# Turning a quad of tokens by a transfer or by TensorE, and a new order of steps

## The chip, the cores and the metric

The kernel runs on one core of one Trainium2 chip. The metric is the device time of one execution in microseconds (us); several executions are timed and the median counts. A profile of one more execution shows what each engine did: TensorE (PE, and PEld for its weight loads), VectorE (DVE), ScalarE (ACT), GpSimd (POOL) and SyncE (SP, which here only issues transfers). PSUM is the memory that matmuls write; SBUF holds everything else on the chip.

## What is computed

An attention block over four batches of 12416 tokens of 128 channels with 32 inducing points, twice (the points attend to the tokens, then the tokens to the 32 results `h`), and a feed-forward layer with a ReLU gate on the tokens.

```
def mab(q, kv):
    s = scale * (q @ kv.transpose(0, 2, 1))
    s = s - s.max(-1, keepdims=True)
    a = np.exp(s)
    a /= a.sum(-1, keepdims=True) + 1e-09
    return a @ kv
h = mab(I, x)                      # I: 32 points for each of 4 batches
x = mab(x, h)                      # (4, 12416, 128), then as (49664, 128)
gate = np.maximum(x @ w_gate, 0.0) # w_gate, w_val: 128 x 1536
val = x @ w_val
out = gate * val @ w_out           # w_out: 1536 x 128
```

## The kernel before

The second attention and the feed-forward layer are folded: since a token's attention output is a mixture of 32 rows of `h`, the layer's output is a quadratic form in its 32 weights `p`. For each batch the kernel makes tables `T` and `L` out of `h` and the weights, and per token it needs only `p`, the squares `F` of differences of pairs of `p`, and matmuls of `F` and `p*p` with the tables. A last check at the end branches to a general kernel, which does not run for these inputs.

A batch has 97 tiles of 128 tokens: six *quads* of 16 tiles and a *rest* of one tile. Each batch has a first phase (needs every token of it once, gives `h` and the tables) and a second (gives the outputs, one block `Q` for a quad).

- First phase of batch 0: `first_batch`, before everything else, about the first 25 us. It loads x as fp32, casts it, turns each group of eight tiles by PE transposes (L336) and copies them out of PSUM on DVE (L337).
- First phase of batches 1 to 3, by quad: `load` (L206, a transfer on POOL's queue that casts to fp16 into one of six buffers `x16q`, or `x16r` for the rest), `turn` (L664, a transposing transfer on SP's queue from `x16q` to one of twelve buffers `xT`), `s1` (scores, PE L673), `p1` (exp, ACT L678), `hz` (weighted sums, PE L688), `ha` (added up, DVE L711). After the rest come `join` and `centre`, which give `h`, then the tables: `gate`, `u` (products `U`, DVE L876), `uj` (their join, L890, DVE or POOL or left to PE), `tm` (PE L895), `tab` (L909 or L907).
- Second phase, by block `Q`: `s2` (PE L472), `p` (exp, ACT L481), `pp` (squared p, L491, DVE or POOL), `z` and `zr`, `zq` (sums and reciprocals), for j = 0 to 3 `d` (differences, 16 matmuls in all, L528), `f2` (squares of two banks, ACT L542) and `fc` (the other two: squared by ACT L554, or cast by DVE L556 and then multiplied, `fm`, L560, by DVE or POOL), then the outputs `o` (PE L568 and L580), `e` (divide into one of four buffers `osb`, DVE L590), and `st` (store, SP L605).

No scheduler runs on the chip: the order is a text, `ORDER`, which names one step after another, its engine where it has several, and the buffer of each ring (`m`, six PSUM banks; `F`, twelve; `xT`; `x16`; `osb`) that it takes. `Plan.run` issues them in that order. Each engine works off its own instructions in this order and waits at each for what it needs; what stands behind on the same engine waits too. SP's queue holds loads of batch 0, turns and stores; POOL's holds the loads of batches 1 to 3. A batch's loads stand on POOL behind `turned` (L660), a copy of one element that waits for the transposing transfers of the batch before. A step `turn` of a quad is allowed only after the turn of the quad before, and quad 0's only after the rest's:

```
before = [("after", "turn", b, q - 1 if q else NQ)] if q < NQ else []
add(("turn", b, q), "SP", [("load", b, q)] + before, xs + xs2, f(turn, q))
add(("s1", b, q), "PE", [("turn", b, q)], xs2 + [p1, ms], f(s1, q))
```

Of the kernel before, what the change touches and what calls it, by code (L numbers as in the profile page):

```python
# [10 lines left out]
FP16 = mybir.dt.float16  # L11
# [5 lines left out]
class Plan:  # L17
# [9 lines left out]
    def add(self, name, engs, deps, uses, fn, unless=None):  # L27
        engs = (engs,) if isinstance(engs, str) else tuple(engs)
        self.steps.append((name, engs, list(deps), list(uses), fn, unless))

    def run(self, text, idle):
# [3 lines left out]
        left = {}  # L35
# [6 lines left out]
        def over(s):  # L42
            for k in s[3]:
                left[k] -= 1
                if not left[k]:
                    used.remove((k[0], self.slot[k]))

        def dropped():
# [25 lines left out]


ORDER = """
Ls00Lt2Lo050q040Lu2Lp2000320r1011Lq2Lz022S011Lw04L-1Lx1Ly1Lr2M12Lv20t05030304202200600030M922T1L+10
810710A1MA2M820ID041BM320K10J10CD020A0u2MF2MB20D10G1MM0MN03MG0MH04ME2MC2MD2MI0MJ00O00509MO00E10M10P
1MP0M230Q2MY0MS0MT02MK00w00158MQ0ML10R30530v3M43MR20y20x1MZ04MU0MV01C00317MW00S10+2Ma0M5001D11G1MX2
0-31E216005261711F2Mb01A21e032Mc0Md1M6210001251221f1M711111810U040V00k031B30s32KE40l02V002W21410m00  # L80
n01q001541r11u10Z001h020o20Jm460W0440300a01330z30b01i24510c01k002531s11g210d230X0Jr471I031l11J01Y01
1o20Y21m21Z02000052Jw481T041a01n31j32112412221b02331p30f02J-490g01U047001c221w005111V01x11y24821+10
h01K00i0K44A0j24931N051W01O0Jn000K94BJo11X21z22e001201L01P01Q0Js0142f12g2Jp001R21Jq21M2Jt12k001592i
11S40e4Ju04Jx00026022B030p42l12m12o2Jy12C04A0051AM022p2Jv22U203G0424C24B1K00104E13H1K11270Jz05J+24D
2K50012Y0054BK61K2002c12Z12D0280K701Me22X2K32KA014K823I222a1KF000KM32902E0KG12q00157KN30KB12A212r12
s12u12M00KT312F2KC04KH022N02O0KD22G4KI23M003482P02H01KJ22Q23KZ322h346313N1KK02Kf332I0KL22J03O13Q13Y
005052-032K03Z13c13a13003102L2320Kl34Kr35Mj04Mq023320Ms1Mr1Mf01Mn00Mk2Mp1Mo1Ml23503360Mg2Mm2Mh23703
e005262w04M-2Mi2Mv2Mw22x03i13f12y03802z03A003J02Mu13g12+23B03C0Mx3Kx33442R43D03S0014239213K23T13L33
E23U13W14SB05334T14U14W1N02Mt2N22My026W0013+013-03v04Mz2N126X1ND23w04G005344I13x04004105i002M+14K1N
724H1NE056Z02NF06a2NI15j1N803N904M00251NC14O13y03p004u0303q0N32N42N62N524Q14N13F4Ky41d44v13r03k023s  # L90
03l03m03z20422KO413n05400537NJ24Y044Z0NP35515814a04b0NK013o23NL05615G003294o05KU40Ka43434NO13t24c21
5H14p04q04r05I15A000105k304d04Kg424s225C24e04w225D34f04g04j035K15B15E14+0052BKm454h25225014-14x004k
0NQ01NR0533KP014NU24y24i4Ks447K0504z2KQ15o002165X005p17L15s24l04m05M045N05q24n25t35u00128KR055O05v1
KV003KS25y25P0KW15w15R055l025Y05Q20Kb0135S0Kc164004155T05m25n25r26826515U05Z0KX025V25z35+00312661KY
25W44t4Kd053u46Y21622Kh0025a05c045-1601Ke2Kn011633Ki16i005335d0Ko15e05f07N026j16m1880126925b216k2Kj
006Q056l3Kk27O28916o0030AKp02Kt0016R06S0L436p16T0L5306s25g25h46u000416U20NV2Kq2Ku16q16L016v17P2Kv03
6M06N06c005246O06y16w16A046g26P2Kw26d1Kz0106B0LB316t36C06D0K+16e17c002196E226V46F007d1LH326h36G06H0
K-037e28y0517g16b3L02L126I07Q0042B8z17R17U17S1L2036J2L3279017A08A32LN33LT347M307B07C07W005007E027D2
38-047F0NW039027a17Y18B007G0Ne01NZ2NX27H07X1913LZ35Na04Nh058C2NY27I27f3Lf3Ng1Nf17300Nb2Nc2Nd27i0031
7Nj1Ni1Nu26+026-07j1700710740Nl375072217608E005457m17k19m0107728F17t027J46K47847u08I17v0Ny28Q003027  # L100
o047w09n18U18G18R17p07z017+07-07q0Nm2Nv2Ns2Nt27r08S19800058800N+3991O40O5037x207s2O60O709C19A18K002
46O808M28L1Lg49p0582008308409q28O18W002518N2Nn2O92850No2N-04L6488123862O008Y18a18X18D3Np03CC022LC47
Nq2Nw2O319K00514CD1Nr19L18s008h048i08j0LI468k0Nz2Nx29M19O1A20023A8t08u08v08n058o0LO498l22OA38p0A31A
61A418w218q0L7001874LU4A9E00403L818c03Lh0129I28r29G19F1L9018d0La4B8e0LA2LD000OG29J38+318f09y00457LE
1OB01Li19+29z17y4LF008x4OC08g2A01LJ0029200439LG2942OF2LK1OH00931OI0CF05Aa021LL04CG29529619s00150Ab1
LM29Q039w29t19u2LP0049R09S0LQ1Ay0025B9v3CH3OL29b01Az1B029T0LR009U239o20LS2A+1Ag004519c0Ah19d09V03Ai
29e0Ad02Ak19x2A8000459W0Ae2AA2AC19X09Y0A91BO050Aj2Ac329Z2Lj02LV0049g00BP1Af29-2AB2Lb013LW19r39h09i0
Lc19j09f20BU00546LX039k2BV1AE01LY28m49a49l4AF0BY2AG0BW1AH0As00032AI21Ld04At1AP05Le2AQ0Nk2Lk2AR0Au1A
m00144Ll2AS0AJ02An1Aq2AK0AT22AL0Ar2B13AM0Bg00048Aw1Ao1Bi2AN2AU05Bh1AV0AW0AX0D0031Bk1Ba00109B702D11B
b1Be1AY2OM2BQ21D230B80B90BI04BA0Bc1Bm00533BJ0BB23Bj2BK0BL0Bn1Bo1Bq1D300BM20BR01B202B30B40D42BS2B50B  # L110
T2D52CU00405BZ3B62Lm01CV1CW2Dq050BC4AO4BD03Ln2Dr1CI00247BE0CY1BF0CE32CX3BG0BH2CK1CJ1CM2OR05OV00ON01
OX1OW1CO00230OO2OS2CN3OY04Bs00OP2OU2OT2CP1Bt0OQ2Bu0Oc3Oa1OZ1CQ2Bv0D60051ACS1Bw23C604C70C102D71Oo2C8
0Ca0030BOj2D81DA1C90C20Cb1C30Ee052CR3C40CA21Ce2Ef1E000144C52Cf3Bx00E11E22CB4Dt05By0Eh02Bz0Cc1Du2B+0
Ok2Ei2Eq00151E41Cl03Cg04Er1B-2Ch0Om2Cm0Eu1Es1DO00202Ci0Oe3DS2Cj0DP1Cn0Co0Cr05Ck21Ol2DQ1DI00103Cw04D
J1Cp2Cx0Cy0Or2Cz0Cs0DK1AZ4C04Cq4DC00239DM1Ct0DG2Cu0DD1Cv22Os01Ot0FS001DE1Dv3Od3DT3Ow2Dw00356Ox0C+2F
# [21 lines left out]
def square_body(ctx, tc, x, inducing, moe_w_gate, moe_w_val, moe_w_out, out):  # L137
    nc = tc.nc
    B, N, C = x.shape
    M = inducing.shape[0]  # L140
    DFF = moe_w_gate.shape[1]
    P = 128
# [5 lines left out]
    NQ = NT // CT  # L148
# [24 lines left out]
    eye16 = const([P, P], FP16, "eye16")  # L173
# [24 lines left out]
    x16q = [const([P, CT, C], FP16, f"x16q{i}") for i in range(NX16)]  # L198
    x16r = [const([P, 1, C], FP16, f"x16r{b}") for b in range(B)]
# [236 lines left out]
    mb = [psum.tile([P, BLK], FP32, name=f"mb{i}") for i in range(NM)]  # L436
# [13 lines left out]
    seen16 = mt([P, 1], FP16, "seen16")  # L450
# [11 lines left out]
    def xT_of(b, q):  # L462
        return xTq[slot["xT", b, q]] if q < NQ else xTr[b]
# [140 lines left out]
        t0 = q * CT + 8 * h  # L604
        nc.sync.dma_start(out=ov[b][:, t0 : t0 + 8, :], in_=o)  # L605

    for Q in range(B * NQ + 1):
        rest = Q == B * NQ
        b, q = divmod(Q, NQ)
# [2 lines left out]
        def f(g, *a, Q=Q):  # L612
            return lambda e: g(Q, *a, e)

        js = range(1 if rest else 4)
        src = [("turn", i, NQ) for i in range(1, B)] if rest else [("turn", b, q)]
# [39 lines left out]
    def load(b, q, e):  # L656
        load_x(b, q, x16q[slot["x16", b, q]] if q < NQ else x16r[b])

    def turned(b, e):
        pool.tensor_copy(out=seen16, in_=xT_of(b, NQ - 1)[:, 0, 0:1])  # L660

    def turn(b, q, e):
        src = x16q[slot["x16", b, q]] if q < NQ else x16r[b]
        nc.sync.dma_start_transpose(out=xT_of(b, q), in_=src.rearrange("p t c -> p (t c)"))  # L664

    def x16_of(b, q):
        return x16q[slot["x16", b, q]] if q < NQ else x16r[b]
# [67 lines left out]
    for b in range(1, B):  # L735
# [4 lines left out]
        for q in range(NQ + 1):  # L740
# [537 lines left out]
```

## Time and profile before

| | us |
|---|---|
| median of 3 executions | 266.23 (264.77 to 266.80) |
| the profiled execution, its own time | 266.63 |
| its span, first to last instruction | 264.8 |
| PE busy | 236.7 |
| DVE busy | 211.8 |
| ACT busy | 207.1 |
| POOL busy | 105.2 |

Busy times are unions over the span, and an engine that is full in one stretch can be idle in another, so views by stretches of time say more than these shares. Matmuls are pipelined, and PE's busy time counts the time until each one's end; it is not a measure of how fast matmuls could follow each other. The second table is of the transfers that matter here.

| transfer | queue | count | us from issue to landing, median |
|---|---|---|---|
| store of an `osb` (512 KB) | SP | 48 | 4.2 |
| load of a quad (512 KB) | POOL | 18 | 13.3 |
| load of a rest (32 KB) | POOL | 3 | 15.3 |
| turn of a quad | SP | 18 | 5.4 |
| turn of a rest | SP | 3 | 3.2 |

### The profile page before, as it was taken

How to read it: one execution, taken by the hardware profiler on the slowest of the kernel's cores; microseconds unless marked ns; L12 is line 12 of the kernel's file. 1: busy time of each engine (PE TensorE's matmuls, PEld its weight loads, DVE VectorE, ACT ScalarE, POOL GpSimd, SP SyncE). 2: the span in 40 equal slices, each digit the busy share in tenths (PEclk: the TensorE clock that was granted, in tenths of full speed). 3: DMA queues.
4: the chain of work that ended last, by engine and by line, in shares of the span. 5: the costliest groups of instructions: out<-in, count | busy, mean ns of one | idle time of the engine just before them, and what ended most of it. 6: DMA issues, size and time to landing. Idle time of an engine off the chain costs nothing.

```text
span 264.8 us, 9054 instructions
## 1 busy us (share of the span) xinstructions
PE 236.7 (89%) x3835; PEld 170.4 (64%) x3835; DVE 211.8 (80%) x439; ACT 207.1 (78%) x382; POOL 105.2 (40%) x132
## 2 busy tenths in 40 slices
PE   6798889997999788689999499999999999999991
PEld 2686367775767566457777367766666767777780
DVE  3656986784899936568999457999999999989993
ACT  3565979788989667379999568899999999989820
POOL 4457337402620715037604443105450774535100
PEclk9999999999999979799999979999999999999998
DMA  7995995999999669999999599922153214454463
GB/s 256 422 412 137 210 213 110 171 188 261 224 242 274 172 161 178 238 255 243 266 255 249 100 178 229 369 93 112 49 231 136 116 79 162 175 223 161 158 244 125
DMA packets 52620, 53.46 MB, mean 202 GB/s; under 512 B 41280, under 2 KB 41952, under 8 KB 52576
## 3 DMA queue, kind: packets, MB, share of 16 engines
q1 hardware_dynamic: 47952, 42.90, 55.6%
q0 software_dynamic: 4576, 9.93, 20.2%
q8 instruction: 31, 0.51, 0.8%
q14 instruction: 13, 0.11, 0.1%
q10 hardware_dynamic: 48, 0.02, 0.1%
HBM read 27.80 MB, written 25.43 MB: 201 GB/s over the span
## 4 chain that ended last, share of the span: by engine, by line
PE 42%; DMA 30%; DVE 17%; SPq 5%; issue 2%; POOL 2%; ACT 1%; DVEq 0%
PE mb L580 20%; DMA x16r<-in_x_dram 12%; DMA xT<-x16q 6%; PE mb L568 5%; SPq L664 5%; DMA x<-in_x_dram 5%; DVE osb L590 5%; DVE U L876 4%; PE dd L528 4%; DMA out_dram<-osb 4%; PE mb L528 4%; DMA w<-in_moe_w_val_dram 3%; PE mb L895 2%; PE mb L673 2%; PE mb L688 2%
## 5 line engine op out<-in xcount | busy, mean ns | idle before, releaser
L580 PE MATMUL mb<-T,F 128*128 128x128 f16 x1552 | 116.0, 222 | 0.0
L542 ACT ACTIVATE F<-dd 128x1024 f16<-128x1024 f32 x97 | 100.1, 1031 | 16.0 <-PE dd L528 8.2
L580 PEld LDWEIGHTS <-F 128*128 128x128 f16 x1552 | 97.3, 99 | 21.1 <-issue 9.4
L590 DVE TENSOR_TENSOR osb<-mb,zr 128x512 f32<-128x512 f32 x97 | 64.6, 682 | 14.2 <-DMA out_dram<-osb 10.2
L554 ACT ACTIVATE F<-mb 128x512 f16<-128x512 f32 x128 | 73.3, 605 | 3.3 <-PE mb L528 1.9
L560 POOL TENSOR_TENSOR F<-F 128x512 f16<-128x512 f16 x40 | 41.8, 1050 | 66.2 <-DVE F L556 55.5
L556 DVE CAST F<-mb 128x512 f16<-128x512 f32 x66 | 44.5, 683 | 11.9 <-PE mb L528 9.0
L528 PE MATMUL mb<-p,diff 32*128 32x512 f16 (+1 forms) x200 | 41.4, 383 | 1.9 <-DVE osb L590 1.8
L528 PE MATMUL dd<-p,diff 32*128 32x512 f16 (+1 forms) x200 | 38.4, 384 | 1.2 <-ACT F L542 1.0
L568 PE MATMUL mb<-L,pp 128*128 128x512 f16 x96 | 37.0, 385 | 0.5 <-DVE F L556 0.2
L491 POOL TENSOR_TENSOR pp<-p 128x512 f16<-128x512 f16 x14 | 16.9, 1209 | 18.8 <-ACT p L481 11.6
L890 POOL TENSOR_TENSOR U<-U,U 128x1536 f16<-128x1536 f16 x4 | 12.4, 3107 | 28.6 <-DVE U L876 28.6
L528 PEld LDWEIGHTS <-diff 32*128 32x128 f16 x400 | 11.9, 91 | 16.8 <-issue 8.3
L895 PE MATMUL mb<-wo,U 128*128 128x128 f16 x264 | 18.7, 220 | 2.8 <-DVE U L890 1.9
L678 ACT ACTIVATE p<-mb 128x512 f16<-128x512 f32 (+1 forms) x21 | 11.2, 550 | 10.8 <-PE mb L673 9.5
L895 PEld LDWEIGHTS <-U 128*128 128x128 f16 x264 | 14.9, 98 | 6.9 <-issue 2.7
L673 PE MATMUL mb<-indT,xT 128*128 128x32 f16 x288 | 10.1, 177 | 8.0 <-DMA xT<-x16q 7.6
L481 ACT ACTIVATE p<-mb 128x512 f16<-128x512 f32 (+1 forms) x25 | 14.9, 598 | 1.5 <-PE mb L472 1.3
L568 PEld LDWEIGHTS <-pp 128*128 128x128 f16 x97 | 9.5, 98 | 8.2 <-issue 7.8
L673 PEld LDWEIGHTS <-xT 128*128 128x128 f16 x288 | 8.8, 96 | 9.1 <-DMA xT<-x16q 8.8
L560 DVE TENSOR_TENSOR F<-F 128x512 f16<-128x512 f16 x26 | 14.0, 545 | 0.1
L337 DVE COPY xT<-xT_ps 128x1024 f16<-128x1024 f16 (+1 forms) x15 | 8.5, 582 | 5.7 <-PE xT_ps L336 5.4
(147 smaller groups left out, 294.9 us busy)
## 6 DMA issues: line engine op xcount, KB each, us to landing
out_dram<-osb SPq DMA_DIRECT2D x48, 512.0 KB, 4.2
x16q<-in_x_dram POOLq DMA_DIRECT2D x18, 512.0 KB, 13.3
x<-in_x_dram SPq DMA_DIRECT2D x9, 512.0 KB, 6.3
x<-in_x_dram SPq DMA_DIRECT2D x6, 256.0 KB, 8.5
w<-in_moe_w_gate_dram SPq DMA_DIRECT2D x1, 768.0 KB, 8.0
w<-in_moe_w_val_dram SPq DMA_DIRECT2D x1, 768.0 KB, 8.6
wo<-in_moe_w_out_dram POOLq DMA_DIRECT2D x1, 384.0 KB, 6.0
xT<-x16q SPq DMA_TRANSPOSE x18, 5.4
```

The source lines that it names most:

```text
L481: act.activation(out=pb[slot["p", Q]][:, 0:w], in_=mb[slot["m", "s2", Q]][:, 0:w], func=AF.Exp, scale=sm_scale / HS,)
L491: engines[e].tensor_tensor(out=p2b[slot["pp", Q]][:, 0:w], in0=a, in1=a, op=ALU.mult)
L528: nc.tensor.matmul(bs[r][:, o], diff[rows, 4 * jj : 4 * jj + 4, :].rearrange("p k m -> p (k m)"), pb[slot["p", Q]][rows, 0:w], start=True, ...
L542: act.activation(out=Fb[slot["F", Q, j]][:, pair(j), :], in_=dd, func=AF.Square, accum_out=None if k is None else spread(Q, k),)
L554: act.activation(out=dst, in_=src, func=AF.Square, **more)
L556: dve.tensor_copy(out=dst, in_=src)
L560: engines[e].tensor_tensor(out=a, in0=a, in1=a, op=ALU.mult)
L568: nc.tensor.matmul(ps, p2b[slot["pp", Q]][:, tok], tab.rearrange("p r c -> p (r c)"), start=True, stop=False,)
L580: nc.tensor.matmul(ps[:, r * P : (r + 1) * P], lhsT, T[r if rest else Q // NQ][:, j, :], start=False, stop=(r, j) == (3, 3),)
L590: dve.tensor_tensor(out=o[:, 4 * (t % 2) : 4 * (t % 2) + 4, :], in0=mb[slot["m", "o", Q, t]].rearrange("p (r c) -> p r c", r=4), in1=zr[:, ...
L673: nc.tensor.matmul(ps[:, t, :], xT_of(b, q)[:, t, :], indT, start=True, stop=True)
L895: nc.tensor.matmul(ps, U[i][:, t, 4 * j : 4 * j + 4, :].rearrange("p k m -> p (k m)"), wo[:, t, :], start=(i, t) == (0, 0), stop=(i, t) == ...
```

## The change

A turn may now be done in either of two ways, and `ORDER` says which. If its engine is SP, it is the transposing transfer as before. If its engine is PE, the step itself issues nothing, and two new pairs of steps follow (one pair for a rest): `tp`, eight PE transposes of the fp16 tiles into one PSUM bank, and `tc`, a copy of this bank to `xT` by DVE or ACT. The steps of the way not chosen are dropped. The rule that set the turns in sequence is gone. `s1` and `s2` wait for the turn, or for its copies; `turned` waits for the last quad of the batch that a transfer turned.

```
-            before = [("after", "turn", b, q - 1 if q else NQ)] if q < NQ else []
-            add(("turn", b, q), "SP", [("load", b, q)] + before, xs + xs2, f(turn, q))
-            add(("s1", b, q), "PE", [("turn", b, q)], xs2 + [p1, ms], f(s1, q))
+            add(("turn", b, q), ("SP", "PE"), [("load", b, q)], xs + xs2, f(turn, q))
+            for i in range(2 if q < NQ else 1):
+                km, no = [("m", "tp", b, q, i)], (("turn", b, q), ("SP",))
+                ptp, ptc = ("tp", b, q, i), ("tc", b, q, i)
+                add(ptp, "PE", [("turn", b, q)], xs + xs2 + km, f(turn_pe, q, i), unless=no)
+                add(ptc, ("DVE", "ACT"), [ptp], xs2 + km, f(turn_copy, q, i), unless=no)
+            add(("s1", b, q), "PE", there(b, q), xs2 + [p1, ms], f(s1, q))
...
     def turn(b, q, e):
-        src = x16q[slot["x16", b, q]] if q < NQ else x16r[b]
-        nc.sync.dma_start_transpose(out=xT_of(b, q), in_=src.rearrange("p t c -> p (t c)"))
+        if e == "SP":
+            src = x16q[slot["x16", b, q]] if q < NQ else x16r[b]
+            nc.sync.dma_start_transpose(out=xT_of(b, q), in_=src.rearrange("p t c -> p (t c)"))
+            by_dma[b] = q
+
+    def eight(b, q, i):
+        n = 1 if q == NQ else 8
+        ps = mb[slot["m", "tp", b, q, i]].bitcast(FP16).rearrange("p (t c) -> p t c", c=P)
+        return slice(8 * i, 8 * i + n), ps[:, 0:n, :]
+
+    def turn_pe(b, q, i, e):
+        ts, ps = eight(b, q, i)
+        for t in range(ts.start, ts.stop):
+            nc.tensor.transpose(ps[:, t - ts.start, :], x16_of(b, q)[:, t, :], eye16)
+
+    def turn_copy(b, q, i, e):
+        ts, ps = eight(b, q, i)
+        if e == "ACT":
+            act.copy(out=xT_of(b, q)[:, ts, :], in_=ps)
+        else:
+            dve.tensor_copy(out=xT_of(b, q)[:, ts, :], in_=ps)
...
     def turned(b, e):
-        pool.tensor_copy(out=seen16, in_=xT_of(b, NQ - 1)[:, 0, 0:1])
+        if b in by_dma:
+            pool.tensor_copy(out=seen16, in_=xT_of(b, by_dma[b])[:, 0, 0:1])
...
-Ls00Lt2Lo050q040Lu2Lp2000320r1011Lq2Lz022S011Lw04L-1Lx1Ly1Lr2M12Lv20t05030304202200600030M922T1L+10
+N000N405N32N1200040N52N22NB03011N62N8010q0220600040NC1N72N91NF2NA1ND10A10710r10810IE051B0J10M10K1NM
```

The new order leaves 12 of the 18 quads to SP's transfers and gives six to PE: quad 2 of batch 1, quads 0, 2, 3 and 4 of batch 2, quad 1 of batch 3. The rests of all three batches go to PE. Of the 15 copies DVE has 14 and ACT one. The order also chooses other engines elsewhere:

| step | before | now |
|---|---|---|
| turn by transfer (SP), rests among them | 21 | 12 |
| `fc` on ACT / DVE | 128 / 66 | 123 / 71 |
| `fm` on POOL / DVE | 40 / 26 | 49 / 22 |
| `pp` on POOL / DVE | 14 / 11 | 22 / 3 |
| `uj` on POOL / DVE | 4 / 6 | 2 / 8 |
| `tab` on ACT / DVE | 6 / 10 | 4 / 12 |
| `lin` on POOL / DVE | 5 / 7 | 8 / 4 |
| `zq` on POOL / DVE | 16 / 9 | 19 / 6 |
| copy of PE's transposes (`tc`) on ACT / DVE | - | 1 / 14 |

SP's queue around the turns of batch 2, before (`xTr2` and `x16r2` are of the rest of batch 2, `x16q0` to `x16q5` hold its quads 0 to 5, `osb` lines are stores):

```order
L605 DMA out_0_dram<-osb1_706 128x1024
L664 DMA_TRANSPOSE xTr2_107<-x16r2_117 128x1x128
L605 DMA out_0_dram<-osb2_707 128x1024
L664 DMA_TRANSPOSE xT1_94<-x16q0_109 128x16x128
L664 DMA_TRANSPOSE xT0_93<-x16q1_110 128x16x128
L664 DMA_TRANSPOSE xT3_96<-x16q2_111 128x16x128
L605 DMA out_0_dram<-osb0_705 128x1024
L664 DMA_TRANSPOSE xT2_95<-x16q3_112 128x16x128
L664 DMA_TRANSPOSE xT5_98<-x16q4_113 128x16x128
L605 DMA out_0_dram<-osb1_706 128x1024
L664 DMA_TRANSPOSE xT4_97<-x16q5_114 128x16x128
```

The same queue at the same place now (the last transfer, from `x16q0`, is quad 0 of batch 3):

```order
L606 DMA out_0_dram<-osb3_708 128x1024
L606 DMA out_0_dram<-osb0_705 128x1024
L672 DMA_TRANSPOSE xT5_98<-x16q1_110 128x16x128
L672 DMA_TRANSPOSE xT4_97<-x16q5_114 128x16x128
L606 DMA out_0_dram<-osb0_705 128x1024
L606 DMA out_0_dram<-osb2_707 128x1024
L606 DMA out_0_dram<-osb1_706 128x1024
L606 DMA out_0_dram<-osb3_708 128x1024
L672 DMA_TRANSPOSE xT6_102<-x16q0_109 128x16x128
```

Of batch 2's seven transfers two are left, side by side, with no store between them; the rest's, which stood first, is gone from the queue.

DVE at the second half of batch 1's tables, before (L876 and L890 make `U`, L590 divides into `osb`):

```order
L876 TENSOR_TENSOR U1_683<-va_677,ga_675 128x12x4x32
L590 TENSOR_TENSOR osb0_705<-mb4_673,zr_702 128x512
L590 TENSOR_TENSOR osb0_705<-mb1_670,zr_702 128x512
L890 TENSOR_TENSOR U0_682<-U0_682,U1_683 128x12x128
L590 TENSOR_TENSOR osb3_708<-mb2_671,zr_702 128x512
L590 TENSOR_TENSOR osb3_708<-mb0_669,zr_702 128x512
L590 TENSOR_TENSOR osb1_706<-mb4_673,zr_702 128x512
L590 TENSOR_TENSOR osb2_707<-mb5_674,zr_702 128x512
L556 CAST F0_690<-mb0_669 128x512
```

The same place now (L690 are the copies of the transposed tiles):

```order
L591 TENSOR_TENSOR osb2_707<-mb2_671,zr_702 128x512
L690 COPY xT0_93<-mb3_672 128x1024
L690 COPY xT3_96<-mb4_673 128x1024
L906 TENSOR_TENSOR U1_683<-va_677,gb_676 128x12x4x32
L690 COPY xT0_93<-mb2_671 128x1024
L591 TENSOR_TENSOR osb3_708<-mb3_672,zr_702 128x512
L507 RECIPROCAL zr_702<-mb5_674 128x16
L591 TENSOR_TENSOR osb0_705<-mb4_673,zr_702 128x512
L690 COPY xT2_95<-mb5_674 128x1024
L690 COPY xT1_94<-mb3_672 128x1024
```

Five copies of eight tiles stand between the divides and the products, and no join: at this place POOL has it.

PE where it first reads what came of the rest of batch 2, before (row 3646 of 7772; L673 are its scores, L580 outputs of a block):

```order
L580 LDWEIGHTS F5_695
L580 MATMUL mb4_673<-T1_87,F5_695 128x128
L673 LDWEIGHTS xTr2_107
L673 MATMUL mb0_669<-indT_156,xTr2_107 128x32
L580 LDWEIGHTS F6_696
L580 MATMUL mb4_673<-T1_87,F6_696 128x128
```

And now (row 2944 of 7970; L683 is the transpose of the rest, L529 the differences of a block, L581 outputs of another):

```order
L529 LDWEIGHTS diff_69
L529 MATMUL mb2_671<-p2_686,diff_69 128x512
L683 LDWEIGHTS x16r2_117
L683 MATMUL mb5_674<-eye16_67,x16r2_117 128x128
L581 LDWEIGHTS F11_701
L581 MATMUL mb1_670<-T0_86,F11_701 128x128
```

PE itself now waits for the landing of the rest's load, some 700 of its rows earlier than it read the turned rest before; its differences and outputs of other blocks stand behind.

More of the change, by code (lines that the diff above doesn't have):

```diff
@@ L44, in over @@
                 left[k] -= 1
-                if not left[k]:
+                if not left[k] and k in self.slot:
                     used.remove((k[0], self.slot[k]))
@@ L82 @@
[L82 to L91, printed above, removed]
@@ L605, in store, with there @@
         nc.sync.dma_start(out=ov[b][:, t0 : t0 + 8, :], in_=o)
+    def there(b, q):
+        return [("turn", b, q)] + [("tc", b, q, i) for i in range(2 if q < NQ else 1)]
     for Q in range(B * NQ + 1):
@@ L615, in square_body @@
         js = range(1 if rest else 4)
-        src = [("turn", i, NQ) for i in range(1, B)] if rest else [("turn", b, q)]
+        src = [i for k in range(1, B) for i in there(k, NQ)] if rest else there(b, q)
         ms, mz, p, pp = ("m", "s2", Q), ("m", "z", Q), ("p", Q), ("pp", Q)
```

96 lines of the change are left out of this document (54 added, 42 removed).

## Prediction

> **What bounds the kernel now.** The page first: no engine is full over the span (PE 89%, DVE 80%, ACT 78%), so the time lies in waits, or in stages with different limits. So I cut the span into stretches where SP issues turns and stretches where it issues none, and read the busy time of each (the view by windows: length, then busy us and count of each engine, granted clock, DMA share, GB/s).
>
> ```profile
> core 0: us, PE busy (x) PEld busy (x) DVE busy (x) ACT busy (x) POOL busy (x), PEclk, DMA share, GB/s
> 54.00:66.00 12.00, 10.30 (x269) 7.67 (x266) 7.84 (x21) 9.75 (x18) 1.22 (x3) 1.00 1.25 221
> 66.00:86.00 20.00, 19.92 (x325) 14.04 (x322) 18.72 (x41) 19.13 (x39) 6.00 (x10) 1.00 1.05 248
> 86.00:120.00 34.00, 26.81 (x458) 19.49 (x456) 21.78 (x38) 21.27 (x37) 12.37 (x12) 0.90 0.95 207
> 120.00:146.00 26.00, 25.66 (x417) 18.61 (x415) 24.04 (x52) 25.18 (x48) 12.43 (x15) 1.00 0.97 244
> 146.00:170.00 24.00, 19.81 (x373) 14.79 (x370) 16.50 (x33) 17.75 (x33) 9.46 (x8) 0.93 1.02 206
> 170.00:184.00 14.00, 14.00 (x220) 9.72 (x218) 12.76 (x31) 12.73 (x24) 2.60 (x3) 1.00 0.30 120
> ```
>
> The reader is to see two kinds of stretch. In 66-86, 120-146 and 170-184 (60 us) DVE is busy 18.72 + 24.04 + 12.76 = 55.5 us (92.5%) and ACT 57.0 (95%): these two are the limit there, and only less work would help. In 54-66, 86-120 and 146-170 (70 us) DVE has 46.1 us (66%) and ACT 48.8 (70%), and in two of them PE's clock falls to 0.90 and 0.93: here something else is the limit. SP's own queue in time names it (start, length, what):
>
> ```profile
> 46.38 16.35 SPq L664 DMA_TRANSPOSE xT<-x16q  x6
> 62.92 15.39 SPq L605 DMA_DIRECT2D out_dram<-osb  x7
> 91.35 2.51 SPq L664 DMA_TRANSPOSE xTr<-x16r  x1
> 93.92 0.57 SPq L605 DMA_DIRECT2D out_dram<-osb  x1
> 94.59 8.98 SPq L664 DMA_TRANSPOSE xT<-x16q  x3
> 103.66 0.53 SPq L605 DMA_DIRECT2D out_dram<-osb  x1
> 104.30 6.27 SPq L664 DMA_TRANSPOSE xT<-x16q  x2
> 110.66 0.94 SPq L605 DMA_DIRECT2D out_dram<-osb  x1
> 111.70 4.35 SPq L664 DMA_TRANSPOSE xT<-x16q  x1
> ```
>
> Six turns of batch 1 hold the queue for 16.35 us, 2.7 us each. From 78.3 (62.92 + 15.39) to 91.35 the queue issues nothing at all, then a rest's turn, then turns between single stores. The views of waits say for what, and who pays (waited for: us, times, longest; SP's from its own view, the others from the whole span):
>
> ```profile
> SPq L664 <- DMA x16r<-in_x_dram: 53.3, 3, 28.8
> DVE osb L590 <- DMA out_dram<-osb: 10.2, 3, 4.5
> PEld L673 <- DMA xT<-x16q: 8.8, 6, 3.9
> POOL seen L660 <- DMA xT<-x16q: 10.8, 1, 10.8
> PE mb L528 <- DVE osb L590: 1.8, 2, 1.0
> ```
>
> SP waits 53.3 us for the three rest loads, the last of each batch's seven, because the rest's turn stands first; the stores behind it come late, and DVE then stands 10.2 us for a free `osb`. PE waits 8.8 us for turns, and POOL 10.8 us for batch 1's last one before it asks for batch 2's loads.
>
> **What the stalls are worth.** At the pace of the quiet stretches (DVE 0.925, ACT 0.951, whichever asks for more) the work of 54-66 takes 9.75/0.951 = 10.3 us, that of 86-120 21.78/0.925 = 23.5, that of 146-170 17.75/0.951 = 18.7. The excess is 1.7 + 10.5 + 5.3 = 17.5 us: the most that better turning can give before any cost.
>
> How much of it comes back, batch by batch, are estimates from the orders above:
> - Batch 2 (86-120): four quads and the rest go to PE, two turns stay, in one place behind two stores; no store stands behind a rest load. The two turns still cost SP 5.4 us, so I take 85%: 8.9 us.
> - Batch 3 (146-170): five of six quads stay with SP, but the rest, for which SP stood still, is PE's, and quad 0's turn stands four stores behind batch 2's last turn, not eight and a rest. 60%: 3.2 us.
> - Batch 1 (54-66): quads 0 and 1 no longer wait for the rest load. 60% of 1.7: 1.0 us. These turns now run beside the loads, on the same DMA engines; if that delays the rest load by as much as five turns (13.5 us), this 1.0 is gone, no more, since its reader moved to PE's queue.
>
> Sum: 13.1 us back.
>
> **What it costs.** Counted from both orders; the rows that price it (by form: busy, mean ns of one):
>
> ```profile
> L337 DVE COPY xT<-xT_ps 128x1024 f16<-128x1024 f16 x9 | 6.1, 689 | 4.7 <-PE xT_ps L336 4.7
> L337 DVE COPY xTr<-xT_ps 128x128 f16<-128x128 f16 x1 | 0.2, 226 | 0.3 <-PE xT_ps L336 0.3
> L556 DVE CAST F<-mb 128x512 f16<-128x512 f32 x66 | 44.5, 683 | 11.9 <-PE mb L528 9.0 <-PE dd L528 2.4
> L560 DVE TENSOR_TENSOR F<-F 128x512 f16<-128x512 f16 x26 | 14.0, 545 | 0.1
> L890 DVE TENSOR_TENSOR U<-U,U 128x1536 f16<-128x1536 f16 x6 | 7.5, 1272 | 0.0
> L491 DVE TENSOR_TENSOR pp<-p 128x512 f16<-128x512 f16 x10 | 5.4, 539 | 0.0
> L834 DVE TENSOR_TENSOR lt<-ga,va 128x384 f16<-128x384 f16 x3 | 1.7, 551 | 0.0
> L909 DVE TENSOR_SCALAR T<-mb,half 128x128 f16<-128x128 f32 x10 | 3.4, 341 | 1.6 <-PE mb L895 1.6
> L511 DVE TENSOR_TENSOR zr<-zr 128x16 f32<-128x16 f32 x9 | 1.9, 223 | 0.1
> L554 ACT ACTIVATE F<-mb 128x512 f16<-128x512 f32 x128 | 73.3, 605 | 3.3 <-PE mb L528 1.9 <-PE dd L528 1.4
> L542 ACT ACTIVATE F<-dd 128x1024 f16<-128x1024 f32 x97 | 100.1, 1031 | 16.0 <-PE dd L528 8.2 <-PE mb L528 6.7
> L560 POOL TENSOR_TENSOR F<-F 128x512 f16<-128x512 f16 x40 | 41.8, 1050 | 66.2 <-DVE F L556 55.5
> L491 POOL TENSOR_TENSOR pp<-p 128x512 f16<-128x512 f16 x14 | 16.9, 1209 | 18.8 <-ACT p L481 11.6
> 176.31 0.89 PE mb L580 x16
> 27.32 16.87 DMA x16r<-in_x_dram
> 131.53 15.31 DMA x16r<-in_x_dram
> ```
>
> (The last three are of the chain in order of time: start, length, what.)
> - DVE: 11 copies of eight tiles at 0.689 and 3 of a rest at 0.226 = 8.3. The new order also moves work: 5 more casts (+3.4), 2 more joins (+2.5), 2 more table outputs (+0.7), 4 fewer squares (-2.2), 8 fewer squared p (-4.3), 3 fewer linear products (-1.7), 3 fewer zq (-0.7). Net +6.1 us, on the engine that is 92.5% busy when nothing stalls: I put all of it on the path. Each copy waits for its eight transposes, and behind it on DVE stand divides and casts, for which PE and SP wait; 5 us of that in all would be the bound, as the row of 10.2 us has three such waits of up to 4.5.
> - ACT: 5 fewer squares at 0.605, 1 copy that I price as the other 128x1024 read of PSUM, 1.03, and small moves: about -2. Taken as nothing, since DVE is the fuller; it is what could make the DVE price smaller.
> - POOL takes 9 squares at 1.05 and 8 squared p at 1.21, some 19 us, and gives back two joins. It is 40% busy and its rows above idle on their producers, so nothing, unless a square comes late to its matmuls.
> - PE: 12 x 8 + 3 = 99 transposes. 16 matmuls of that width take 0.89 us in the chain, 56 ns each: 5.5 us. A PE that reads 100% in a quiet stretch is not at this pace (its matmuls have a mean of some 220 ns, started 56 ns apart), and it has 7.2 us idle in 86-120: taken as 0, bounds 0 and 5.5.
> - PSUM: 15 more holds of a bank out of six. The one row where PE waits for a bank that DVE is late to empty is 1.8 us: 0 taken, 0 to 1.8 the bound.
>
> **The sum.** -13.1 + 6.1 = -7.0. The profiled execution took 266.63 us (span 264.8); 259.6 by it. The median before, 266.23, is 0.4 lower: 259.2.
>
> A rule against this: the Trainium skill (Advanced Engine Details and Errata, X-Bar Transpose (TRN2)) says that transposing transfers are as fast as plain ones, at 350-400 GB/s. By that a quad of 0.52 MB would take an estimated 1.4 us, not the 2.7 that the row of six shows, and taking turns off SP would free half as much. The trace speaks against the rule here.
>
> **Rivals.**
> - *Everything comes back* (0.20). All 17.5 us return, and half of DVE's 6.1 hides where DVE still waits: -14.4, 251.8. For it: the wait for the rest, 53.3 us, leaves SP in all three batches. Against: five turns of batch 3 still queue.
> - *The turns weren't what fills the transfers* (0.18). In 86-120 the DMA engines are 95% busy with loads and stores as well. If only half of my 13.1 comes back, DVE's price eats it: -6.5 + 6.1 = -0.4, 265.8, no change. For it: 66-86 has a share of 1.05 and runs well, so a full share is not slow by itself, and something else may pace 86-120. Half is also what the page's rule above would give.
> - *PE waits instead of SP* (0.12), the slower side. A rest's load is the last of seven and lands 15.3 to 16.9 us after its issue. SP could stand for it; PE's queue holds the scores, differences and outputs of every block, and the order has PE read `x16r2` some 700 rows earlier than before. If PE stands 6 us for it in batches 2 and 3 each, 13.1 shrinks to 1.1, and with DVE's 6.1 the time is +5.0: 271.2. It decides once PE's new waits pass 13.1 - 6.1 + 2.7 = 9.7 us. Against: fewer transfers are queued ahead of the load than before.
> - My forecast, 0.50: 256 to 263.5.
>
> **Numbers.** One per cent (2.7 us) is about what a measurement of this kernel can tell from no change. Faster than 263.6: 0.50 + 0.20 = 0.70; within 1%: 0.18; slower: 0.12. The range runs from 251 (the best case) to 267 (most of the no-change case): some 0.8 of the chance.
>
> **What would show it.** Right: SP's wait for x16r near 0; DVE's wait for `out_dram<-osb` under 3 us; the granted clock at 1.00 where it was 0.90; DVE busy some 6 us more in a shorter span. Batch 2's scores follow PE's copies without a gap. Wrong: PE or PEld waiting at the new transposes for `x16q` or `x16r` by more than 5 us; casts or divides waiting for the copies; DVE at 95% with no time gained (the price is bigger than 6.1); or batch 3's scores still waiting for `xT<-x16q` as before.

## The result, and the profile after

| | before | after |
|---|---|---|
| median, us | 265.88 (264.77 to 266.80, 4 runs) | 255.96 (254.91 to 260.03, 4 runs) |
| ratio to before | | 0.9616, 95% interval 0.9559 to 0.9672 |
| the profiled execution, us | 266.63 | 256.14 |
| its span | 264.8 | 254.3 |
| DVE busy + idle in the span | 211.8 + 53.0 | 216.8 + 37.5 |

The change makes the kernel 3.8% faster, by 9.9 us; 7.0 were forecast. Some executions of a kernel run a few per cent longer at a lower granted clock (260.03 is one); medians count them and ratios leave them out, so where the two differ, as for e2 below (259.72 to 276.18), the ratio is the one to compare. The last row splits this in the manner of the prediction: DVE does 5.0 us more work and stands idle 15.5 us less. The page's first part has the busy times:

```profile
span 254.3 us, 9242 instructions
PE 235.2 (92%) x3932; PEld 173.4 (68%) x3932; DVE 216.8 (85%) x444; ACT 206.6 (81%) x377; POOL 124.5 (49%) x152
```

The same stretches of time as in the prediction, by windows of the kernel after (length, then busy us and count of each engine, granted clock, DMA share, GB/s). Work has moved earlier in time, so a row does not hold the same steps as before, but it shows how full the engines are there:

```profile
54.00:66.00 12.00, 12.00 (x314) 9.40 (x310) 8.24 (x21) 11.67 (x22) 8.38 (x12) 1.00 0.99 227
66.00:86.00 20.00, 18.34 (x292) 13.74 (x281) 16.80 (x36) 15.57 (x31) 6.68 (x9) 0.91 0.86 212
86.00:120.00 34.00, 34.00 (x652) 26.29 (x649) 30.43 (x62) 30.33 (x54) 16.84 (x18) 1.00 0.91 204
120.00:146.00 26.00, 24.19 (x387) 17.88 (x387) 24.82 (x45) 23.44 (x44) 16.77 (x18) 1.00 0.84 201
146.00:170.00 24.00, 24.00 (x487) 17.75 (x483) 21.85 (x46) 22.20 (x39) 8.36 (x10) 1.00 0.75 193
```

In 86-120 DVE goes from 21.78 to 30.43 us and the clock from 0.90 to 1.00; in 146-170 DVE goes from 16.50 to 21.85. These were the stretches in which something else was the limit. Not every stretch gained: in 66-86 DVE now has 16.80 us where it had 18.72, and the clock reads 0.91 instead of 1.00. SP's queue in time, of the kernel after (start, length, what):

```profile
31.31 23.92 SPq L672 DMA_TRANSPOSE xT<-x16q  x5
55.46 33.50 SPq L606 DMA_DIRECT2D out_dram<-osb  x8
89.06 7.69 SPq L672 DMA_TRANSPOSE xT<-x16q  x2
99.22 2.92 SPq L606 DMA_DIRECT2D out_dram<-osb  x4
110.29 6.17 SPq L672 DMA_TRANSPOSE xT<-x16q  x1
117.35 23.26 SPq L606 DMA_DIRECT2D out_dram<-osb  x7
140.72 12.41 SPq L672 DMA_TRANSPOSE xT<-x16q  x4
```

Batch 2's two turns (89.06) stand between groups of stores, and no rest's turn is left. The waits of the kernel after that answer to those in the prediction (waited for: us, times, longest; the last row is SP's own):

```profile
DVE osb L591 <- DMA out_dram<-osb: 3.0, 2, 2.0
PE mb L529 <- DVE osb L591: 2.6, 4, 1.6
POOL seen L667 <- DMA xT<-x16q: 1.9, 1, 1.9
SPq L672 <- DMA x16q<-in_x_dram: 23.6, 2, 15.5
```

SP's wait for rests, 53.3 us before, is gone. It still stands 23.6 us for loads of quads, but DVE's wait for a free `osb` falls from 10.2 to 3.0. The new instructions, and the scores they feed, in the view of groups by form (busy, mean ns of one, idle time before it and what ended it):

```profile
L699 PE MATMUL mb<-indT,xT 128*128 128x32 f16 x288 | 9.8, 176 | 0.0
L690 DVE COPY xT<-mb 128x1024 f16<-128x1024 f16 x11 | 7.2, 669 | 0.5 <-PE mb L683 0.5
L683 PE MATMUL mb<-eye,x16q 128*128 128x128 f16 x96 | 6.6, 219 | 0.0
```

PE no longer waits before the scores (its weight loads waited 8.8 us for turns before), and DVE's copies wait 0.5 us for their transposes. Apart from 66-86 this is as forecast, with the 3.0 us for `osb` at the bound that was given. It doesn't show which of three things brought it: the rests by PE, the six quads by PE, or the new order.

### The profile page after: what moved, and what is told of

Same layout as the page of the kernel before. It is cut to its first block, busy times and chain, and to the rows that moved or that the text cites. A ratio compares the mean times of both kernels' runs of the same rounds, so it can differ in the third digit from the quotient of the medians.

```text
span 254.3 us, 9242 instructions
## 1 busy us (share of the span) xinstructions
PE 235.2 (92%) x3932; PEld 173.4 (68%) x3932; DVE 216.8 (85%) x444; ACT 206.6 (81%) x377; POOL 124.5 (49%) x152
## 4 chain that ended last, share of the span: by engine, by line
PE 64%; DVE 21%; DMA 8%; issue 3%; ACT 1%; SPq 0%; POOL 0%; DVEq 0%; POOLq 0%
PE mb L581 25%; DMA out_dram<-osb 8%; PE mb L569 7%; DVE U L906 6%; DVE osb L591 5%; PE mb L529 5%; PE dd L529 4%; PE mb L925 4%; PE mb L699 3%; PE xT_ps L337 2%; DVE F L557 2%; PE mb L683 2%; PE mb L714 2%; PE mb L473 2%; PE warm_ps L282 1%
## 5 line engine op out<-in xcount | busy, mean ns | idle before, releaser
L581 PE MATMUL mb<-T,F 128*128 128x128 f16 x1552 | 113.8, 220 | 0.0
L581 PEld LDWEIGHTS <-F 128*128 128x128 f16 x1552 | 96.1, 98 | 20.5 <-issue 9.2
L561 POOL TENSOR_TENSOR F<-F 128x512 f16<-128x512 f16 x49 | 52.6, 1085 | 63.6 <-DVE F L557 58.2
L555 ACT ACTIVATE F<-mb 128x512 f16<-128x512 f32 x123 | 71.2, 605 | 5.3 <-PE dd L529 3.3
L591 DVE TENSOR_TENSOR osb<-mb,zr 128x512 f32<-128x512 f32 x97 | 64.6, 680 | 10.2 <-PE mb L581 6.0
L557 DVE CAST F<-mb 128x512 f16<-128x512 f32 x71 | 47.8, 680 | 5.2 <-PE mb L529 2.5
L529 PE MATMUL mb<-p,diff 32*128 32x512 f16 (+1 forms) x200 | 39.8, 377 | 4.7 <-DVE osb L591 2.6
L529 PE MATMUL dd<-p,diff 32*128 32x512 f16 (+1 forms) x200 | 37.7, 378 | 0.9 <-ACT F L543 0.6
L492 POOL TENSOR_TENSOR pp<-p 128x512 f16<-128x512 f16 (+1 forms) x22 | 24.6, 1123 | 11.3 <-PE mb L569 5.9
L529 PEld LDWEIGHTS <-diff 32*128 32x128 f16 x400 | 11.4, 91 | 18.7 <-issue 9.6
L512 POOL TENSOR_TENSOR zr<-zr 128x16 f32<-128x16 f32 x19 | 7.5, 394 | 11.6 <-DVE zr L507 11.6
L347 POOL CAST x16f<-x 128x512 f16<-128x512 f32 (+2 forms) x15 | 8.4, 562 | 9.5 <-DMA x<-in_x_dram 8.9
L337 PE MATMUL xT_ps<-eye,x16f 128*128 128x128 f16 x97 | 8.9, 234 | 1.8 <-DVE x16f L344 1.1
L207 POOL DMA_DIRECT2D x16q<-in_x_dram x18 | 10.1, 571 | 0.9 <-PE mb L723 0.4
```

The lines of the kernel that those rows point to most:

```text
L492: engines[e].tensor_tensor(out=p2b[slot["pp", Q]][:, 0:w], in0=a, in1=a, op=ALU.mult)
L529: nc.tensor.matmul(bs[r][:, o], diff[rows, 4 * jj : 4 * jj + 4, :].rearrange("p k m -> p (k m)"), pb[slot["p", Q]][rows, 0:w], start=True, ...
L555: act.activation(out=dst, in_=src, func=AF.Square, **more)
L557: dve.tensor_copy(out=dst, in_=src)
L561: engines[e].tensor_tensor(out=a, in0=a, in1=a, op=ALU.mult)
L581: nc.tensor.matmul(ps[:, r * P : (r + 1) * P], lhsT, T[r if rest else Q // NQ][:, j, :], start=False, stop=(r, j) == (3, 3),)
```

## The experiments

Twelve kernels. *Old order* is the order of the kernel before, *new order* that of the kernel after. Times are medians; ratios are to the kernel before on the same chip (265.7 to 265.9 us each time).

| kernel | order | rests turned by | quads turned by PE | us | ratio, 95% interval |
|---|---|---|---|---|---|
| before | old | SP, first | 0 | 265.88 | 1 |
| after | new | PE | 6 | 255.96 | 0.9616 [0.9559, 0.9672] |
| e1 | old | SP, last | 0 | 266.57 | 1.0021 [0.9991, 1.0051] |
| e7 | old, one rest's scores late | SP, last | 0 | 257.05 | 0.9679 [0.9645, 0.9712] |
| e7b | old | PE | 0 | 254.17 | 0.9558 [0.9520, 0.9597] |
| e9 | old | PE | 4 | 260.86 | 0.9787 [0.9731, 0.9842] |
| e6 | old | PE | 6 | 266.13 | 1.0003 [0.9971, 1.0035] |
| e2 | new | PE | 0 | 264.67 | 0.9813 [0.9769, 0.9857] |
| e8 | new, SP's queue sorted by hand | PE | 0 | 266.16 | 0.9987 [0.9946, 1.0028] |
| e3 | new | SP, late | 6 | 256.59 | 0.9685 [0.9626, 0.9743] |
| e4 | after, copies twice | PE | 6 | 262.53 | 0.9848 [0.9776, 0.9919] |
| e5 | after, PE transposes twice | PE | 6 | 262.45 | 0.9845 [0.9791, 0.9899] |
| r1 | after again | PE | 6 | 256.42 | 0.9606 [0.9558, 0.9654] |
| r2 | e7b again | PE | 0 | 254.56 | 0.9557 [0.9515, 0.9598] |

### Only the place of the rests' turns (e1)

SP's queue, batch 2; likewise for batch 1, and in batch 3 behind quad 4's turn:

```diff
-L664 DMA_TRANSPOSE xTr_107<-x16r_117 128x1x128
 L605 DMA out_dram<-osb_707 128x1024
 L664 DMA_TRANSPOSE xT_94<-x16q_109 128x16x128
...
 L664 DMA_TRANSPOSE xT_97<-x16q_114 128x16x128
+L664 DMA_TRANSPOSE xTr_107<-x16r_117 128x1x128
```

> The kernel before, with its order unchanged but for SP: each rest's turn stands behind quad 5's (in batch 3 behind quad 4's) and no longer ahead of quad 0's. Every turn stays a transfer, nothing moves on another engine. Theory (SP stood for the rest loads, and turns and stores stood behind it): SP's wait for x16r, 53 us before, falls under 15, the osb wait of 10.2 us falls under 5, and the time is 259 to 262. Rival (the transfers' own time paces the three stretches, PE is needed to take them over): 264 to 267.

No gain: 266.57, as the rival had it, though the waits moved as the theory had it: SP no longer waits for `x16r`, and DVE's wait for `osb` falls from 10.2 to 3.7 us. So it isn't that nothing happened. The step `centre` of batch 2 starts at 122.8 us where it started at 128.3 before, as early as in the kernel after (122.6). Then batch 3 takes it back. Waits of e1:

```profile
PEld L673 <- DMA xTr<-x16r: 9.9, 1, 9.9
PE mb L673 <- DMA xTr<-x16r: 9.7, 1, 9.7
```

In the old order, batch 3's scores of the rest stand on PE right behind those of quad 1, which made sense while the rest was turned first. Now PE stands there until the rest's turn, the last but one of the batch in SP's queue, has landed, 9.9 us in one piece. The wait had moved from SP to PE.

### The same, with batch 3's rest scored late (e7)

Here batch 3's rest is turned behind quad 5, not quad 4. PE's queue; the exponential on ACT and the rest's weighted sums move with it:

```diff
 L580 MATMUL mb_672<-T_87,F_691 128x128
-L673 LDWEIGHTS xTr_108
-L673 MATMUL mb_671<-indT,xTr_108 128x32
...
 L697 MATMUL mb_672<-ones_75,p_0_703 128x1
+L673 LDWEIGHTS xTr_108
+L673 MATMUL mb_670<-indT,xTr_108 128x32
```

> The kernel before with the rests' turns last in SP's queue, as in e1, and in batch 3 the rest's scores, exponential and sums put behind those of quad 5, so that PE does not stand for a turn that comes last; nothing is turned by PE. e1 was 5.5 us ahead at batch 2's end (centre 2 at 122.8 against 128.3) and lost it again where PE stood 9.9 us at the rest's scores of batch 3. Theory (the old order lost time only where a queue stood for a rest, on SP before and on PE in e1): the 5.5 us stay and batch 3 adds some 2 to 3, so 257 to 261; PE's wait at the scores for xTr under 2 us, DVE's wait for out_dram<-osb under 4. Rival (batch 3's turns come late anyway, because they stand behind stores, and PE waits for the next one instead): the gain is lost in batch 3 again, 264 or more, with PE waiting at the scores for xT<-x16q.

257.05, ratio 0.9679: the fast edge of the theory's range. DVE waits 3.1 us for `osb`, PE not for the rest any more, though 5.0 us for turns of quads. Not one instruction is added, nothing is turned by PE, and of the order three turns and one rest's steps have moved. That alone brings 8.7 us (265.74 - 257.05).

### Only the rests by PE (e7b)

The old order; three `tp` and three `tc` put in, the rests' turns out of SP's queue:

```diff
-L664 DMA_TRANSPOSE xTr_107<-x16r_117 128x1x128
...
+L682 LDWEIGHTS x16r_117
+L682 MATMUL mb_671<-eye_67,x16r_117 128x128
```

> The kernel before, its order kept, with the three rests alone turned by TensorE (3 transposes and 3 small copies), the eighteen quads all by SP. Theory of the prediction (SP standing for the rest loads holds up turns and stores): the same work as before plus 0.7 us of DVE, without the 53.3 us that SP stood: 257 to 261, SP waiting for x16r not at all, DVE for out_dram<-osb under 4 us. Rival (the wait moves to PE, where the rests' transposes stand among the scores of the other quads): 263 or more, PE waiting for x16r by 5 us or more. Second rival (transfers are full anyway): 263 or more without any such wait, the turns of quads landing no earlier.

254.17, ratio 0.9558: more than the theory's 257 to 261, and not above the kernel after. The page's first part, and two windows, of e7b:

```profile
PE 232.0 (92%) x3838; PEld 167.9 (66%) x3838; DVE 212.6 (84%) x442; ACT 206.9 (82%) x382; POOL 105.0 (41%) x132
```

```profile
86.00:120.00 34.00, 31.09 (x570) 22.76 (x568) 28.21 (x53) 29.02 (x52) 18.38 (x19) 1.00 1.12 237
146.00:170.00 24.00, 23.10 (x421) 17.02 (x421) 20.67 (x46) 20.88 (x36) 5.78 (x7) 1.00 0.69 194
```

DVE's work is up by 0.8 us, its idle time down from 53.0 to 40.4 (span 253.0 less 212.6). In 86-120 the DMA engines carry more than before (share 1.12, 237 GB/s, against 0.95 and 207), and all six quads of batch 2 are still turned by transfers, and yet DVE gets 28.21 us of work done there instead of 21.78. Waits of e7b:

```profile
PEld L698 <- DMA xT<-x16q: 1.8, 3, 1.4
DVE osb L590 <- DMA out_dram<-osb: 1.1, 2, 0.6
```

With eighteen turns on SP and no queue standing for a rest, PE's weight loads wait 1.8 us for turns and DVE 1.1 us for `osb`.

### The six quads by PE as well, old order (e6), or four of them (e9)

e6 is e7b with the change's six quads turned by PE, each copy on DVE seven to fifteen steps of `ORDER` ahead of its scores (in the kernel after, nine of the twelve stand 58 to 104 steps ahead); e9 has only batch 2's four.

```diff
-turn (2,0)  SP
+turn (2,0)  PE
+tp (2,0,0)  PE
+tc (2,0,0)  DVE
+tp (2,0,1)  PE
+tc (2,0,1)  DVE
```

> The order before with one thing of the change: the same six quads and the three rests are turned by PE, the copies all by DVE, put some 10 to 20 steps ahead of the scores that need them, in banks that are free there; all else stands as before. Theory (turning off SP's queue is what brings the gain): the osb wait is under 4 us and the time 256 to 261, DVE paying 8.3 us for its copies. Rival (the new order's balance of the other steps brings it): 263 or more.

> The kernel of e7b with batch 2's quads 0, 2, 3 and 4 turned by TensorE as in e6, and quads of batches 1 and 3 left with SP. e6, which has two quads more on PE, took 12.0 us more than e7b; between centre 2 and 3 batch 2 took 56.4 us in e6 and 49.8 in e7b. Theory (a quad on PE costs its 16 transposes, 0.9 us, and its two copies, 1.4, each on the path): 4 x 1.6 to 2.3, so 260 to 263. Rival (the price is of something single in e6, a bank or a place in the order): within 3 us of e7b, or as much as e6 already, 265 and more.

e6: 266.13, nothing gained over before, as the rival had it. Against e7b, which it is but for the six quads, that is 12.0 us lost; by the ratios 11.8, give or take 1.1 (the half-widths of both, taken as independent). e9: 260.86, in the range of the theory; 6.7 us lost by the medians, 6.1, give or take 1.8, by the ratios. So a quad on PE, placed as it is here, costs 1.5 to 2.0 us of the whole time. Its own work is two copies and 16 transposes, 2 x 0.669 + 16 x 0.056 = 2.2 us. The page of e6:

```profile
PE 239.4 (91%) x3934; PEld 174.1 (66%) x3934; DVE 219.8 (83%) x454; ACT 207.6 (79%) x382; POOL 104.1 (39%) x132
```

DVE has 7.2 us more work than in e7b, and idles 44.7 us (span 264.5) instead of 40.4.

### The new order without the quads on PE (e2, e8), and with the rests by SP (e3)

e2 gives the six quads of the kernel after back to SP, at the places in the order at which their `turn` steps stand. e8 also moves each store in SP's queue right behind its last divide, and batch 3's second turn and batch 2's turns, but for quad 1's, later. e3 gives only the rests back.

```diff
-turn (2,0)  PE
-tp (2,0,0)  PE
-tc (2,0,0)  DVE
-tp (2,0,1)  PE
-tc (2,0,1)  DVE
+turn (2,0)  SP
```

> The changed kernel and its order, but the six quads given to PE are turned by SP's transfers again, at the places where their turns stand in the order; the rests stay with PE, the twelve copies of eight tiles are gone. Theory (the place in SP's queue was the trouble, not the transfers): within 3 us of the changed kernel, 253 to 259, since the 7.6 us of copies go as well. Rival (the transfers pace it, PE had to take six): 261 or more, with osb or xT waits of 5 us and over.

> The order of e2 (the new order, all eighteen quads by SP, the rests on PE) with SP's own queue sorted: each store right behind its last divide, batch 2's turns and batch 3's second one later, about where their loads land. In e2 SP stood 23.1 us for two loads with stores behind, and DVE waited 9.5 us for a free osb. Theory (e2 lost its 4.9 us to the kernel after by stores behind standing turns, not for want of PE's turning): osb wait under 3 us and 251 to 256, at or under the kernel after. Rival (the new order needs its quads earlier than SP can turn them): 258 or more, with PE waiting at the scores for xT<-x16q by 5 us or more.

> The changed kernel and its order, but the three rests are turned by SP's transfers, at the place of PE's turn. Theory: in the new order the rest's turn stands late, after most turns, so SP waits little for it: 255 to 258. Rival (any rest on SP's queue stops turns and stores): 260 or more, and SP's wait for x16r is over 15 us.

e3 is 0.6 us above the kernel after by the medians, and by the ratios 2.0, give or take 1.8, above the mean of its two measurements: where the order puts the rests late enough, it matters little who turns them. e2 is 5.4 us slower than the kernel after (0.9813 against 0.9611, the mean of its two measurements), nearer to the rival than to the theory. Waits of e2:

```profile
DVE osb L590 <- DMA out_dram<-osb: 9.5, 4, 4.4
PE mb L528 <- DVE osb L590: 5.5, 4, 4.0
```

DVE stands for free `osb` again. The chain that ended last shows three of the stores that it stood for (start, length until the landing, what):

```profile
70.86 9.42 DMA out_dram<-osb
101.64 5.19 DMA out_dram<-osb
126.86 12.88 DMA out_dram<-osb
```

Only the second stood behind turns, three of them, until 101.54 us. The first and the third were issued with no turn just ahead of them, the first as its divides ended, and took 9.42 and 12.88 us to land, against a median of 4.2 in the kernel before. So the place in SP's queue is one part of these waits and slow landings are the other; why they landed so late no run here shows. That e8 would mend this was wrong: 266.16, slower still. Its waits, from an execution of 269.87 us:

```profile
DVE osb L590 <- DMA out_dram<-osb: 13.9, 4, 4.2
PEld L698 <- DMA xT<-x16q: 1.9, 2, 1.1
```

Neither theory holds for e8 (the profiled execution is the longest of ten, so its waits tell only the kind). The rival had the time, but wanted PE to wait 5 us or more for turns, and it waits 1.9. The four stores that DVE stood for took 5.4 to 8.4 us to land here, once more longer than 4.2; what made e8 slower stays open. What is shown is only that the new order, in the two ways tried, is slower with all quads on SP; whether some order of SP's queue would do without PE, stays open.

### What the copies and the transposes cost in the kernel after (e4, e5)

```diff
-            dve.tensor_copy(out=xT_of(b, q)[:, ts, :], in_=ps)
+            for _ in range(2):
+                dve.tensor_copy(out=xT_of(b, q)[:, ts, :], in_=ps)
```

```diff
-        for t in range(ts.start, ts.stop):
+        for t in 2 * list(range(ts.start, ts.stop)):
             nc.tensor.transpose(ps[:, t - ts.start, :], x16_of(b, q)[:, t, :], eye16)
```

> The kernel after, with each DVE copy of turned tiles out of PSUM done twice: 11 copies of 0.689 and 3 of 0.226 more, some 8.3 us of DVE, and no other change; the second copy writes the same values. The prediction put the copies' whole price on the path. Theory (DVE sets the pace): 255.96 + 7 to 8 = 263 to 264, DVE busy about 225. Rival (DVE has 37.5 us idle in the kernel after, and the copies lie in it): under 259, DVE's idle time down by 5 us or more.

> The kernel after, with each PE transpose of a quad's or a rest's tile done twice into the same place of PSUM: 99 transposes of 128 columns more, 5.5 us at 56 ns each, nothing else. The prediction priced PE's transposes at nothing. Theory (a PE that reads as busy is waiting on others): 255 to 257.5. Rival (PE, 64 per cent of the chain of work that ended last, sets the pace): 260 to 262.

The pages of e4 and of e5, in this order:

```profile
PE 236.1 (91%) x3932; PEld 173.3 (67%) x3932; DVE 223.6 (86%) x458; ACT 207.3 (80%) x377; POOL 124.5 (48%) x152
```

```profile
PE 240.0 (92%) x4031; PEld 178.2 (69%) x4031; DVE 216.6 (83%) x444; ACT 206.8 (80%) x377; POOL 123.9 (48%) x152
```

By the ratios, against the mean of the two measurements of the kernel after: the second set of copies costs 6.3 us, give or take 2.1, for 8.3 us of work as priced and 6.8 us more of DVE's busy time: nearer the theory (7 to 8) than the rival (under 3). The second set of transposes costs 6.2, give or take 1.7, for 5.5 us as priced and 4.8 us more of PE's busy time: the rival, just past its range. DVE sets the pace with most of its work, as taken, but PE does too, and its transposes were priced at nothing. One way in which they reach the path is seen at the copies of e5 (0.5 us of idle time in the kernel after):

```profile
L690 DVE COPY xT<-mb 128x1024 f16<-128x1024 f16 x11 | 7.4, 676 | 3.3 <-PE mb L683 3.3
```

DVE waits 2.8 us longer for a bank of transposes that takes PE twice as long. Doubling thus measures the work together with this delay, not the work alone.

### After and e7b on one chip (r1, r2)

No edit: the kernel after and e7b, five rounds each.

> The kernel after, unchanged, beside r2 on one chip. Theory now (the gain is that of the rests; the six quads on PE and the new order together bring nothing beside it): this is 0.960 to 0.964 of before, and r2 at or below it. Rival (the quads on PE add to the gain): this is below r2 by more than the intervals.

> The kernel of e7b unchanged (the kernel before, its order kept, with the three rests alone turned by TensorE), beside r1 on one chip. Theory now: 0.953 to 0.960 of before, 1 to 2.5 us under r1. Rival: e7b's 254.17 was chance, and this is at r1's time or above.

256.42 and 254.56, in the ranges of the theory. e7b is 1.8 and 1.9 us under the kernel after in the two pairs of medians, with intervals that overlap in each pair; both pairs together, by the means of the ratios, say 1.4 us, give or take 1.2. So the best kernel of this study is the kernel before with three PE transposes and three small copies: 0.9557, and the rest of the change adds nothing to it that these runs can show.

## Why the prediction was right, and where it wasn't

The direction held, and so did the main mechanism, SP standing for the rests; what the quads on PE and the new order do was wrong. The time lies within the range, and just past the fast edge of the forecast's own (256 to 263.5). Its steps:

- **SP standing for the rests is the cause.** Shown, and more sharply than the prediction had it: e7 moves nothing but rests and has 8.7 of the 9.9 us; e7b has 11.6.
- **13.1 us back.** e7b is this term by itself: DVE's idle time falls by 12.6 us. By batches the prediction had 1.0, 8.9 and 3.2; by the starts of the three `centre` steps and the end, e7b has 0.2, 7.8 and 4.0, and r2, the same kernel in another execution, 0.8, 4.1 and 5.3. The sums, 12.0 and 10.2, lie near each other; the splits don't.
- **"four quads and the rest go to PE, two turns stay".** This is the step that failed in its reason. It gave the quads a share in what comes back. e7b gets all of it back with all the quads on SP.
- **DVE +6.1, all on the path.** Measured +5.0; and e4 shows that some three quarters of the price of the copies turn into time (6.3, give or take 2.1, of 8.3). Right in kind, a little too much in size. DVE's copies waited 0.5 us, with 5 as the bound.
- **PE's 99 transposes "taken as 0, bounds 0 and 5.5".** Wrong as far as e5 tells: a second set of them costs 6.2 us, give or take 1.7, near the upper bound, though with the delay that it puts on the copies. The reason given, that matmuls can start 56 ns apart where PE reads as full, says that there is room in PE's pace, not that the work behind is not late: the transposes stand in a queue whose later rows DVE and ACT wait for. That this is how they cost time is argued, and seen only at the copies of e5.
- **The new order priced by the work that it moves, -2.2 of DVE.** Mis-sized. From e6 to the kernel after, the same turns done by the same engines (but for one copy on ACT), the time falls by 10.2 us (266.13 - 255.96); DVE's work is 3.0 of it (219.8 to 216.8), its idle time 7.2 (44.7 to 37.5). The sum of the case by runs: rests -11.6, quads on PE +12.0, order -10.2; together -9.8. The prediction had -13.1, +8.3 for the copies (0.7 of it for the rests', so the match of terms is rough) and -2.2 for moved work. The quads and their copies were 3.7 too small, the order 8.0, the rests 1.5 too large; the errors of opposite sign left 2.8 us of difference. That the forecast came so near was in this part luck. How the 12.0 and the 10.2 divide depends on where e6 puts the transposes and copies in an order that was not searched for them; their sum, +1.8, and the -11.6 don't.
- **POOL's 19 us free, ACT at nothing, PSUM at nothing.** POOL is busy 19.3 us more and ACT 0.5 less. PE waits 2.6 us for banks behind `osb` (1.8 before). As taken.
- **The rivals.** Everything back: no; even e7b, with the cost of the quads away, is at 254.2, not 251.8. Transfers full anyway: no; e7b's 86-120 has them fuller, and the work flows (in the new order with all quads on SP, where stores land late, this is not settled). PE waits for the rest instead of SP: not in the kernel after, nor in e7b, whose PE turns the rests in the old order and never waits for `x16r`. In e1 PE does stand, 9.9 us at one instruction, and the gain is gone; but there it waits for the rest's turn, which stands late in SP's queue, and not for the load. The rival had the kind of wait right and the place wrong.
- **The rule of the Trainium skill (Advanced Engine Details and Errata, X-Bar Transpose (TRN2)) on turns as fast as plain transfers.** It would have made the turns worth half. As the turns themselves turned out not to be what was lost, no run settles it. The row of four in the profile after, 12.41 us, doesn't either: 7.1 us of it are waits for PE. Its five turns of quads that waited for nothing held SP's queue for 2.1 to 4.3 us each, nearer the 2.7 of the prediction than 1.4.

Open: which of the many moves in the new order bring its 10.2 us. No run here takes it apart; the gain of e6 to after is spread over all batches (start of the first `centre` 73.6 to 69.4, then 56.4 to 53.2, 53.0 to 51.6 and 81.6 to 80.1 us).

## What to carry to other kernels

When a queue stands for a late load, first try to move only the instruction that stands, on every engine that has one (SP's turn and PE's scores here): three turns and one rest's scores, exponential and sums, moved in e7, brought 8.7 of the 9.9 us that a new way of turning and a new order brought together. A wait that is taken off one queue is found again at the next reader that kept its early place. And price work on an engine that reads as full at its full time, even when its instructions could overlap; doing the work twice is a quick test of it, which counts what the work delays as well.

## What the runs showed of the hardware

The kernel of e7b was profiled twice; the stretch from the first `centre` to the second took 49.8 us in one execution and 53.5 in the other (r2). The windows of r2 show why (columns as before, each 4 us):

```profile
102.00:106.00 4.00, 4.00 (x103) 3.06 (x103) 3.83 (x8) 4.00 (x8) 0.96 (x1) 1.00 1.17 255
106.00:110.00 4.00, 1.89 (x43) 1.35 (x40) 1.42 (x3) 2.65 (x5) 0.08 (x1) 0.89 1.18 182
110.00:114.00 4.00, 4.00 (x72) 2.70 (x64) 1.98 (x5) 1.90 (x4) 3.43 (x6) 0.50 1.05 397
114.00:118.00 4.00, 3.94 (x54) 2.17 (x53) 2.18 (x6) 2.85 (x6) 0.38 (x1) 0.75 0.96 153
118.00:122.00 4.00, 3.86 (x53) 2.61 (x51) 3.74 (x8) 3.81 (x8) 3.60 (x6) 1.00 1.05 265
```

and PE's waits in that part of r2:

```profile
PE mb L713 <- DVE osb L590: 2.1, 1, 2.1
```

PE stood 2.1 us once, for a bank behind a divide, and then the granted clock was 0.89, 0.50 and 0.75 for three windows, with DVE and ACT half idle behind it. In e7b's first execution that wait is missing and the clock is 1.00 throughout the stretch. The Trainium skill (TensorE: Matmul & The Clock Gate, Why this matters for your kernels) asks for no idle gaps of PE over some 3 us; here a gap of 2.1 us went ahead of a half clock. That the gap caused it, rather than came with it, is what the order of the rows suggests; no run here tried it by itself. The length of the gap alone doesn't decide. After one and the same wait of PE for `U`, 1.9 us, the clock of the next window (92 to 96) was 0.69 in e9 and 1.00 in e7b, and after a wait of 2.6 us (from 79.7) it stayed at 1.00 in e5. If gaps bring it about, that would explain why a stall of 2 us can cost more than 2 us, and why the split by batches differs between two executions of one kernel.
